# Choosing and loading the first experts one to two steps earlier in a chain of linear attention

## The chip, the cores and the metric

One Trainium2 chip; the kernel runs on one of its cores. The time is the device time of one execution in microseconds (us), the median of a few runs. TensorE (PE) multiplies, VectorE (DVE), ScalarE (ACT) and GpSimd (POOL) do the rest, SyncE (SP) issues most of the DMAs; each of them works through a queue of its own in program order.

## The reference

Three stages follow each other. The first is a linear attention with a state (a delta rule) over 4 batches, 8 heads, 768 tokens and 48 channels; the second sends each of its 3072 rows to one of 8 experts; the third is a dense layer with three inputs and a maximum.

```
for t in range(S):
    y[:, :, t] = einsum('bhd,bhde->bhe', q[:, :, t], state)
    v_old = einsum('bhde,bhd->bhe', state, kt)
    state = state + bt * einsum('bhd,bhe->bhde', kt, vt - v_old)
...
e_idx = argmax(x @ w_gate, axis=1)
out[mask] = gate_w * eom[mask, e] * (maximum(x[mask] @ w1[e], 0) @ w2[e])
...
h = maximum(maximum(x @ w1, x @ w2), x @ w3); return h @ w_out
```

## The kernel before

**The chain.** The attention goes over the tokens in 24 steps of 32 tokens for all heads and batches. A step first multiplies keys and queries with the state (`c_ks`, `c_qs`), takes R = scaled values minus the product on VectorE (L321), multiplies R with a small triangular inverse TT (`c_u`), copies the result from PSUM to Ubd on ScalarE and VectorE (L348, L350), updates the state (`c_s`) and copies it to Sbd (L367, L369); only then can the next step begin. In the texts R(21) is the start of L321 in step 21. The values of step i+2 are scaled on GpSimd at the end of step i (`vscale`, L308): it needs the load of TT(i+2) and of kv(i+2) and stands in GpSimd's queue behind whatever was put there before.

**Routing beside the chain.** Every four steps give 512 rows. Their logits, the choice of an expert and the place in the expert's list are worked out in the steps that follow (`r_g`, L417 to L437, with four additions to the running count `cum` on GpSimd, L433; `r_p`, L445 to L467). Then four indirect DMAs, `r_s` (L474), scatter row number, weight and token into a table in DRAM. Each of them waits on GpSimd until the one before has landed, since both write `tab`.

**Experts ahead of time.** After 12 steps the two experts with most rows so far are taken as the first (`first`, ten small operations on VectorE); their numbers are read into SP registers (`first_values`, L805). SP then loads the raw weights in thirds of 128x1024 numbers (0.5 MB): w1 of the first expert, its w2, and w1 of the second (`raws`, L680). GpSimd splits each third or quarter into a high and a low part with a cast (L696) and a subtraction (L697). SP reads the first 256 list entries of each of the two experts (`lists`, L824; this waits for the scatters), and GpSimd gathers 2 x 128 rows for each (`rows`, L840). Near the end of the chain these rows are turned (`turn`, L855) and multiplied (`m1`); the multiplications of the expert stage then follow without a gap. The raw tile of the second expert's w1 uses the same buffer as that of the first expert's w2, so its load waits until the last quarter of that is split.

**What sets the order.** A table of numbers in `ahead`: the whole part of a number is a step of the chain, its fraction the place within the step. The list is sorted and merged into the step's instructions; the scaling of values comes at the end of a step, behind all of that.

```
fl += [lambda: s.loadT(i + 2), lambda: s.vscale(i + 2)]
```

Of the kernel before, what the change touches and what calls it, by code (L numbers as in the profile page):

```python
# [22 lines left out]
def merge(*lists):  # L23

    items = []
    for li, l in enumerate(lists):
        n = len(l)
        for j, f in enumerate(l):
            items.append(((j + 0.5) / n, li, j, f))
    items.sort(key=lambda t: t[:3])  # L30
    return [t[3] for t in items]


class Attn:
# [9 lines left out]
    def __init__(s, ctx, tc, psum, big, hp, gp, kqt, knv, bt, wgt, xd, tab, ctab, cum, ident, wrm, x2):  # L44
        s.tc, s.nc, s.psum, s.big, s.hp, s.gp = tc, tc.nc, psum, big, hp, gp
        nc = tc.nc
        s.kqt, s.knv, s.btd, s.wgtd, s.xd, s.tab, s.ctab, s.cum = kqt, knv, bt, wgt, xd, tab, ctab, cum
        s.ident, s.wrm, s.ones, s.x2 = ident, wrm, wrm[:, 0:128], x2
        s.NI = 24
        s.NP = 12  # L50
        s.NSL = 6
        s.RLB = "m"
        s.XB, s.xTs, s.RLK = 1, {}, 0
        s.CUT = 0.95
        s.NL = 4
        s.NA = 20
        s.LATE = 0.4
        s.W = (0, 1, 0)
        s.END = 13
        s.TU, s.TB, s.MF = (22.92, 22.95, 22.97), "TRT", 2  # L60

        s.BUD = (5.0, 5.6, 4.6, 5.0)

        s.ORD = {0: 0, 1: 14, 2: 36, 3: 50, 4: 66, 5: 80}
        s.prep = (2.8, 2.2, 1.5, 0.6)
        cp = s.cp = ctx.enter_context(tc.tile_pool(name="acst", bufs=1))
        s.p2 = ctx.enter_context(tc.tile_pool(name="ap2", bufs=2))
        s.dr = ctx.enter_context(tc.tile_pool(name="adr", bufs=1, space=DRAM))
        nc.scalar.preload_act_table_set("natural_log_exp_and_others")
        s.chain = False  # L70
        s.RT, s.RD, s.LT = (15.4, (15.9, 0.3), (17.4, 0.35), (21.8, 0.25)), 0.5, ((18.2, 0.45), (19.3, 0.35), (23.0, 0.05))
        s.KQT, s.AT, s.Gd, s.kv, s.TT, s.x, s.inv = {}, {}, {}, {}, {}, {}, {}

    def consts(s):
# [413 lines left out]
    def run(s, pre, tail):  # L488
        nc, NI, NP = s.nc, s.NI, s.NP
        for i in range(s.NL):  # L490
            s.loadKQ(i)
        s.consts()
        s.warm(9)
        A = [lambda p=p, j=j: s.prods(p, j) for p in range(NP) for j in range(2)]
        for k in range(4):
            A[k]()
        s.inv_load(0)
        for f in (s.inv_n1, s.inv_n2, s.inv_n3):
            f(0)
        B = [u[2] for u in s.steps(s.ORD)[:30]]  # L500
        s1 = s.ORD[1]
        for f in merge(B[:s1 // 3], [A[4], A[5]]) + merge(B[s1 // 3:s1 // 2], [A[6], A[7]]):
            f()
        s.inv_load(1)
        s.inv_n1(1)
        for f in merge(B[s1 // 2:s1], [A[8], A[9], lambda: s.inv_n2(1), A[10], lambda: s.inv_n3(1)]):
            f()
        for f in merge(B[s1:], [lambda: s.load32(0), A[11], lambda: s.inv_load(2), s.empty, lambda: s.load32(1)] + A[12:s.NA]):
            f()
        s.inv_end(0)  # L510
        s.warm(8, s.inv[0]["tt"])
        s.inv_store(0)
        s.vscale(0)
        s.vscale(1)

        spr = [[] for _ in range(NI + 1)]
        put = lambda t, f: spr[int(t + 1)].append(((t + 1) % 1, f))
        t, left = [-1.0], [s.BUD[0]]
        s.ends = []

        def take(c):
            while left[0] < c:
                t[0] = int(t[0]) + 1.0 if t[0] >= 0 else 0.0
                left[0] += s.bud(int(t[0]))
            left[0] -= c
            b = s.BUD[0] if t[0] < 0 else s.bud(int(t[0]))
            t[0] = (int(t[0]) if t[0] >= 0 else -1) + min(0.99, max(0, 1 - (left[0] + c) / b))
        for starts in (s.ORD,):
            for st, c, f, en in s.steps(starts)[30:]:
                take(c)  # L530
                put(t[0], f)
                for sl in st:
                    t0 = t[0]
                    for dt, g in zip(s.prep, (s.inv_load, s.inv_n1, s.inv_n2, s.inv_n3)):
                        if sl > 2:
                            put(t0 - dt, lambda g=g, sl=sl: g(sl))
                        elif sl == 2 and g != s.inv_load:
                            put(-1 + (t0 + 1) * (0.3, 0.5, 0.9)[(s.inv_n1, s.inv_n2, s.inv_n3).index(g)], lambda g=g: g(2))
                    s.ends.append(("start", sl, t0))
                for sl in en:  # L540
                    take(1.4)
                    put(t[0], lambda sl=sl: s.inv_end(sl))
                    assert t[0] + s.LATE < 4 * sl - 1, (sl, t[0])
                    put(t[0] + s.LATE, lambda sl=sl: s.inv_store(sl))
                    s.ends.append((sl, t[0]))
        for k, f in enumerate(A[s.NA:]):
            put(0.05 + k * 0.45, f)
        for t, f in pre(s):
            put(t, f)
        s.chain = True  # L550
        for i in range(-1, NI):
            sp = [f for _, f in sorted(spr[i + 1], key=lambda x: x[0])]
            if i < 0:
                for f in sp:
                    f()
                continue
            q, k = i // 4 - 1, i % 4
            x0 = [lambda: s.r_g(q)] if q >= 0 and k == 1 else [lambda: s.r_p(q)] if q >= 0 and k == 2 else []
            f1 = [lambda: (s.x_store(i - 1), s.r_t(i - 1))] if i else []
            f2 = [lambda: s.r_l(q)] if q >= 0 and k == 0 else []  # L560
            s.load32(i + 2)
            if i >= 7:
                s.r_s({19: [0, 1], 20: [2, 3], 21: [], 22: [], 23: [0, 1]}.get(i, [(i - 7) % 4]))
            n = round(len(sp) * s.CUT) if i < 20 else sum(t < s.CUT for t, _ in spr[i + 1])
            wm = lambda k: [lambda: s.warm(s.W[k])]
            fl = [lambda: s.c_ks(i), lambda: s.c_qs(i)] + x0 + wm(0) + merge([lambda: s.c_u(i)] + f1, sp[:n]) + wm(1)
            fl += [lambda: s.c_s(i)] + merge([lambda: s.c_y(i)] + f2, sp[n:]) + wm(2)
            fl += [lambda: s.loadT(i + 2), lambda: s.vscale(i + 2)]
            for f in fl:
                f()  # L570
        tail(s)
# [54 lines left out]
class Moe:  # L626
# [397 lines left out]
    def ahead(s, a):  # L1024

        G = s.nc.gpsimd
        v = {}

        def later(key, n, t, d):
            def go(j):  # L1030
                if (key, n) not in v:
                    v[key, n] = s.split(key, n, G, G)
                v[key, n][j]()
            return [(t + d * j, lambda j=j: go(j)) for j in range((3, 4)[n])]

        def lists():
            s.ids(0)
            s.ids(1)

        def rows(k):  # L1040
            for c in range(2):
                s.gather(k, c)

        def turned():
            z = [a.p2.tile([128, 1024], F32R, tag="Z", name=f"xT0{j}", bufs=4) for j in range(2)]
            s.xT[0] = [tuple(z[c // 2][:, (c % 2 * 2 + j) * 256:(c % 2 * 2 + j) * 256 + 256] for j in range(2)) for c in range(3)]

        def turn(c):
            if c == 0:
                turned()  # L1050
            s.xpose(0, c, a.TB[c])
        def raws(key, n, slot, t, d):
            us = s.raws(key, n, lambda: s.btile(slot, f"r{n}_{key}", F32), 3)
            return [(t + d * j, u) for j, u in enumerate(us)]
        out = [(a.RT[0], s.first), (a.RT[0] + a.RD, s.first_values), (19.3, s.parts), (21.0, lists),
               (21.3, lambda: rows(0)), (21.6, lambda: rows(1))]
        for (key, n, slot), (t, d) in zip(((0, 0, 0), (0, 1, 1), (1, 0, 1)), a.RT[1:]):
            out += raws(key, n, slot, t, d)
        for (key, n), (t, d) in zip(((0, 0), (0, 1), (1, 0)), a.LT):
            out += later(key, n, t, d)  # L1060
        out += [(t, lambda c=c: turn(c)) for c, t in enumerate(a.TU)]
        out += [(23.1 + 0.1 * f, lambda f=f: s.m1(0, f)) for f in range(a.MF)]
        return out
# [207 lines left out]
```

## Time and profile before

| | |
|---|---|
| Time, median of 3 runs (lowest to highest) | 845.05 us (841.39 to 845.97) |
| The profiled execution: its own time, its span | 841.33 us, 839.6 us |
| Busy PE, DVE, ACT, POOL | 88%, 56%, 35%, 27% of the span |
| Mean granted TensorE clock | 0.93 |

The span is counted from the first to the last instruction. The chain's steps 0 to 23 lie in the first third, to about 273 us; behind it TensorE is nearly always busy. The granted clock is a share of TensorE's full speed, so 1.00 is the upper of its two levels and 0.50 the lower.

### The profile page before, as it was taken

To read this page: it belongs to the slowest core of one execution; us is meant where nothing else is said; L and a number is where in the kernel's file an instruction comes from. 1 tells how busy PE (TensorE), PEld (TensorE's weight loads), DVE (VectorE), ACT (ScalarE), POOL (GpSimd) and SP (SyncE) were. 2 spreads that over 40 slices of the span, in tenths; PEclk is the share of its full clock that TensorE was granted. 3 is DMA by queue.
4 is the path that set the end of the run, shared out by engine and by line. 5 is a ranking of instruction groups with operands and counts; after the bars stand their busy time and mean duration, and the time that the engine had idled before them with its cause. 6 is when DMAs were issued, how large, how long until landed. Compare 5 with 4: busy or idle time off the path is not lost. (4 is left out here: it accounts for less than half of the span.)

```text
span 839.6 us, 20331 instructions
## 1 busy us (share of the span) xinstructions
PE 742.9 (88%) x8506; PEld 635.5 (76%) x8517; DVE 471.0 (56%) x1164; ACT 297.2 (35%) x675; POOL 228.5 (27%) x322
## 2 busy tenths in 40 slices
PE   6746877878776986999899999999999999999996
PEld 4634554555554986999899999889898898988886
DVE  3998999986544532788677795452322313233130
ACT  2213666664342331555354453222221221212111
POOL 5666456422688322034032100001001010100101
PEclk7557899999997999899899999999999999999998
DMA  8894544447634235677766697542010020000001
GB/s 218 214 218 122 144 125 121 102 126 202 169 73 140 85 77 150 235 252 221 250 207 229 235 318 269 196 185 85 10 47 29 1 76 0 29 10 10 28 1 41
DMA packets 86045, 110.28 MB, mean 131 GB/s; under 512 B 53893, under 2 KB 67148, under 8 KB 83388
## 3 DMA queue, kind: packets, MB, share of 16 engines
q1 hardware_dynamic: 57547, 87.08, 33.7%
q10 hardware_dynamic: 19360, 11.42, 5.7%
q0 software_dynamic: 9040, 10.42, 4.1%
q8 instruction: 69, 1.13, 0.6%
q14 instruction: 29, 0.23, 0.1%
HBM read 79.53 MB, written 29.36 MB: 130 GB/s over the span
## 5 line engine op out<-in xcount | busy, mean ns | idle before, releaser
L867 PE MATMUL pm<-xhm,wm 128*128 128x512 f32 x648 | 204.7, 395 | 0.0
L940 DVE TENSOR_TENSOR work<-work,pm 128x512 f32<-128x512 f32 x72 | 49.5, 688 | 175.2 <-PE pm L867 175.2
L867 PEld LDWEIGHTS pm<-xhm,wm 128*128 128x128 f32 x648 | 121.8, 188 | 29.1
L867 PE MATMUL pm<-xlm,wm 128*128 128x512 f32 x324 | 128.1, 396 | 0.0
L953 POOL DMA_INDIRECT out_dram<-work,idm x24 | 23.6, 985 | 332.3 <-ACT work L952 318.0
L840 POOL DMA_INDIRECT xg<-xd,ids x32 | 44.1, 1377 | 142.7 <-PE pt L855 122.1
L942 ACT CAST hmh<-work 128x512 fp32r<-128x512 f32 x36 | 22.4, 621 | 154.3 <-DVE work L940 154.3
L239 DVE TENSOR_TENSOR zt<-Z 128x30 f32<-128x30 f32 (+14 forms) x219 | 73.2, 373 | 3.2 <-POOL Z L218 2.6
L867 PE MATMUL pz<-wm,hmh 128*128 128x384 f32 x320 | 73.7, 334 | 0.0
L867 PEld LDWEIGHTS pm<-xlm,wm 128*128 128x128 f32 x324 | 60.9, 188 | 14.4
L245 DVE TENSOR_TENSOR Z<-Z,zt 128x30 f32<-128x30 f32 (+14 forms) x219 | 69.0, 355 | 0.0
L348 ACT COPY Ubd<-pU 32x192 f32<-32x192 f32 x148 | 45.8, 309 | 62.1 <-PE pU L340 50.2
L360 PE MATMUL pS<-Ubd,kv 128*48 128x192 f32 x368 | 42.8, 363 | 17.9 <-ACT Ubd L348 13.9
L867 PEld LDWEIGHTS pz<-wm,hmh 128*128 128x128 f32 x320 | 57.2, 188 | 0.5
L164 PE MATMUL pg<-KQT 48*32 48x64 f32 x1536 | 40.6, 291 | 18.6 <-DMA KQT<-in_kqt_dram 16.1
L164 PEld LDWEIGHTS pg<-KQT 48*32 48x32 f32 x1536 | 34.5, 151 | 25.9 <-issue 12.2
L360 PEld LDWEIGHTS pS<-Ubd,kv 128*48 128x48 f32 x368 | 22.9, 133 | 37.8 <-ACT Ubd L348 22.9
L902 ACT COPY y<-po 128x256 f32<-128x256 f32 (+6 forms) x30 | 13.3, 445 | 75.7 <-PE po L867 74.1
L367 ACT COPY Sbd<-pS 48x384 f32<-48x384 f32 x72 | 34.0, 472 | 12.0 <-PE pS L360 10.3
L859 DVE TENSOR_TENSOR xl<-pt,xh 128x256 fp32r<-128x256 f32 (+6 forms) x27 | 14.0, 520 | 42.2 <-ACT xh L858 33.2
L867 PE MATMUL pz<-wm,hml 128*128 128x384 f32 x112 | 37.4, 334 | 0.0
L891 ACT ACTIVATE hh<-ph 128x440 fp32r<-128x440 f32 (+5 forms) x48 | 23.8, 503 | 27.0 <-PE ph L867 26.5
(302 smaller groups left out, 1615.1 us busy)
## 6 DMA issues: line engine op xcount, KB each, us to landing
raw<-in_w_dram SPq DMA_DIRECT2D x12, 1536.0 KB
kv<-in_knv_dram SPq DMA_DIRECT2D x24, 384.0 KB
wd<-work SPq DMA_DIRECT2D x24, 384.0 KB
wm<-wd SPq DMA_DIRECT2D x8, 1152.0 KB
KQT<-in_kqt_dram ACTq DMA_DIRECT2D x20, 448.0 KB
xd<-x SPq DMA_DIRECT2D x24, 192.0 KB
r<-in_w_dram SPq DMA_DIRECT2D x9, 512.0 KB
raw<-x SPq DMA_DIRECT2D x6, 768.0 KB
```

The costliest lines, as they stand in the source:

```text
L164: nc.tensor.matmul(ps[b * 32:b * 32 + 32, o:o + 64], kq[:, 0, :], kq.rearrange("p k t -> p (k t)"), start=True, stop=True, tile_position=( ...
L239: nc.vector.tensor_mul(t, Z[:, a:e, m].unsqueeze(2).to_broadcast([128, e - a, n]), Z[:, m, m + 1:].unsqueeze(1).to_broadcast([128, e - a, n]))
L245: nc.vector.tensor_add(Z[:, a:e, m + 1:], Z[:, a:e, m + 1:], t)
L348: nc.scalar.copy(dst, src)
L360: nc.tensor.matmul(s.pS[q][j * 64:j * 64 + 48, g2 * 192:g2 * 192 + 192], s.kv[i][:, 0, h, :], s.Ubd[h // 4][:, h % 4, :], start=(i == 0 an ...
L367: nc.scalar.copy(dst, src)
L840: s.nc.gpsimd.indirect_dma_start(t[0:r.ct], None, s.xd[0:2049] if k < 2 else s.xd, bass.IndirectOffsetOnAxis(s.gid[k][0:r.ct, c, 0:1], 0))
L867: s.nc.tensor.matmul(ps, a, b, start=(start and k == 0), stop=(stop and k == n - 1))
L891: nc.scalar.activation(hi, ps, AF.Relu)
L940: nc.vector.tensor_max(m, m, ps)
L942: nc.scalar.copy(hi, m)
L953: nc.gpsimd.indirect_dma_start(s.out, bass.IndirectOffsetOnAxis(i[:, c, 2:3], 0), y, None, bounds_check=3071, oob_is_err=False)
```

## The change

Only numbers of the table change, and the list of scatters by step. `first` goes from 15.4 to 14.2, `first_values` from 15.9 to 14.7 (RT's first number and RD). The raw thirds of w1 go from 15.9 to 14.8, those of w2 from 17.4 to 16.0, those of the second expert's w1 from 21.8 to 19.0. Their splits (LT) go from 18.2, 19.3 and 23.0 to 16.1, 17.3 and 21.0. The count of rows goes from 19.3 to 18.3, the lists from 21.0 to 20.4, the gathers from 21.3 and 21.6 to 20.8 and 21.2. The four scatters of the fourth routing, two each in steps 19 and 20 before, are all issued in step 19.

```diff
--- before.py
+++ after.py
@@ -68,7 +68,7 @@
         s.dr = ctx.enter_context(tc.tile_pool(name="adr", bufs=1, space=DRAM))
         nc.scalar.preload_act_table_set("natural_log_exp_and_others")
         s.chain = False
-        s.RT, s.RD, s.LT = (15.4, (15.9, 0.3), (17.4, 0.35), (21.8, 0.25)), 0.5, ((18.2, 0.45), (19.3, 0.35), (23.0, 0.05))
+        s.RT, s.RD, s.LT = (14.2, (14.8, 0.3), (16.0, 0.25), (19.0, 0.25)), 0.5, ((16.1, 0.4), (17.3, 0.35), (21.0, 0.2))
         s.KQT, s.AT, s.Gd, s.kv, s.TT, s.x, s.inv = {}, {}, {}, {}, {}, {}, {}
 
     def consts(s):
@@ -560,7 +560,7 @@
             f2 = [lambda: s.r_l(q)] if q >= 0 and k == 0 else []
             s.load32(i + 2)
             if i >= 7:
-                s.r_s({19: [0, 1], 20: [2, 3], 21: [], 22: [], 23: [0, 1]}.get(i, [(i - 7) % 4]))
+                s.r_s({19: [0, 1, 2, 3], 20: [], 21: [], 22: [], 23: [0, 1]}.get(i, [(i - 7) % 4]))
             n = round(len(sp) * s.CUT) if i < 20 else sum(t < s.CUT for t, _ in spr[i + 1])
             wm = lambda k: [lambda: s.warm(s.W[k])]
             fl = [lambda: s.c_ks(i), lambda: s.c_qs(i)] + x0 + wm(0) + merge([lambda: s.c_u(i)] + f1, sp[:n]) + wm(1)
@@ -1052,8 +1052,8 @@
         def raws(key, n, slot, t, d):
             us = s.raws(key, n, lambda: s.btile(slot, f"r{n}_{key}", F32), 3)
             return [(t + d * j, u) for j, u in enumerate(us)]
-        out = [(a.RT[0], s.first), (a.RT[0] + a.RD, s.first_values), (19.3, s.parts), (21.0, lists),
-               (21.3, lambda: rows(0)), (21.6, lambda: rows(1))]
+        out = [(a.RT[0], s.first), (a.RT[0] + a.RD, s.first_values), (18.3, s.parts), (20.4, lists),
+               (20.8, lambda: rows(0)), (21.2, lambda: rows(1))]
         for (key, n, slot), (t, d) in zip(((0, 0, 0), (0, 1, 1), (1, 0, 1)), a.RT[1:]):
             out += raws(key, n, slot, t, d)
         for (key, n), (t, d) in zip(((0, 0), (0, 1), (1, 0)), a.LT):
```

The first place is GpSimd's queue at steps 18 to 20, from the scaling of kv20 to that of kv21 and one row on (kv and TT bear the step's number, w1_0 is the first expert's w2, tab the table, xg0 gathered rows). Before:

```order
L308 TENSOR_TENSOR kv20_4240<-kv20_4240,TT20_4380 128x384
L474 DMA tab_78<-rdat3_4290,rpos3_4299 25600x3 x2
L696 CAST w0_0h_4344<-r0_0_3938 128x1024
L697 TENSOR_TENSOR w0_0l_4345<-r0_0_3938,w0_0h_4344 128x1024
L696 CAST w1_0h_4473<-r1_0_4203 128x768
L697 TENSOR_TENSOR w1_0l_4474<-r1_0_4203,w1_0h_4473 128x768
L308 TENSOR_TENSOR kv21_4383<-kv21_4383,TT21_4509 128x384
```

With the change:

```order
L308 TENSOR_TENSOR kv20_4255<-kv20_4255,TT20_4398 128x384
L474 DMA tab_78<-rdat3_4305,rpos3_4314 25600x3 x4
L308 TENSOR_TENSOR kv21_4401<-kv21_4401,TT21_4519 128x384
L840 DMA xg0_0_4612<-xd_76,ids0_4602 128x384
L840 DMA xg0_1_4614<-xd_76,ids0_4602 128x384
```

The pieces of splitting between kv20 and kv21 are gone from here (all of them stand before kv20 now), and four scatters stand there in place of two.

The second place is the same queue at steps 20 to 23 (w0_1 is the second expert's w1, cum the running count, xg1 the rows of the second expert). Before:

```order
L308 TENSOR_TENSOR kv22_4512<-kv22_4512,TT22_4643 128x384
L433 TENSOR_TENSOR cum_74<-cum_74,rohb4_4698 128x8 x4
L840 DMA xg0_0_4754<-xd_76,ids0_4708 128x384
L840 DMA xg0_1_4756<-xd_76,ids0_4708 128x384
L840 DMA xg1_0_4758<-xd_76,ids1_4710 128x384
L840 DMA xg1_1_4760<-xd_76,ids1_4710 128x384
L308 TENSOR_TENSOR kv23_4646<-kv23_4646,TT23_4795 128x384
L459 COPY rdat4_4845<-xrow_199 128x4
L460 COPY rdat4_4845<-tok_194 128x4
L474 DMA tab_78<-rdat4_4845,rpos4_4854 25600x3 x2
L696 CAST w0_1h_4985<-r0_1_4769 128x1024
L697 TENSOR_TENSOR w0_1l_4986<-r0_1_4769,w0_1h_4985 128x1024
```

With the change:

```order
L308 TENSOR_TENSOR kv22_4522<-kv22_4522,TT22_4655 128x384
L433 TENSOR_TENSOR cum_74<-cum_74,rohb4_4710 128x8 x4
L696 CAST w0_1h_4720<-r0_1_4443 128x1024
L697 TENSOR_TENSOR w0_1l_4721<-r0_1_4443,w0_1h_4720 128x1024
L840 DMA xg1_0_4766<-xd_76,ids1_4604 128x384
L840 DMA xg1_1_4768<-xd_76,ids1_4604 128x384
L308 TENSOR_TENSOR kv23_4658<-kv23_4658,TT23_4805 128x384
```

The pair of cast and subtraction stands twice more between the last gather and the scaling of kv23 (left out here). All three thirds of the second expert's w1 are thus split ahead of kv23, where they stood behind it.

The third place is SP's queue at steps 14 to 16 (r0_0 is the raw w1 of the first expert, x the rows that the chain stores). Before:

```order
L302 DMA TT16_3830<-td4_172 128x8x33
L294 DMA kv17_3833<-in_knv_dram 128x768
L805 TENSOR_LOAD early_92 x2
L384 DMA xd_76<-x14_3828 128x384
L680 DMA r0_0_3938<-in_w1_dram 128x1024
L302 DMA TT17_3964<-td4_172 128x8x33
L294 DMA kv18_3967<-in_knv_dram 128x768
```

With the change:

```order
L805 TENSOR_LOAD early_92 x2
L384 DMA xd_76<-x13_3692 128x384
L680 DMA r0_0_3824<-in_w1_dram 128x1024
L302 DMA TT16_3850<-td4_172 128x8x33
L294 DMA kv17_3853<-in_knv_dram 128x768
L384 DMA xd_76<-x14_3848 128x384
L302 DMA TT17_3966<-td4_172 128x8x33
L294 DMA kv18_3969<-in_knv_dram 128x768
```

Two more thirds of r0_0 stand on the two sides of x14 (left out). TT16 moved behind the read of the experts' numbers and the first raw third, and TT17 behind all three thirds instead of one.

## Rows read from the trace of the kernel before

**Rows 1.** Busy time by step of the chain, from one R to the next, all engines.
```profile
202.34:209.43 7.09, 6.07 (x188) 4.42 (x177) 3.08 (x7) 3.31 (x9) 1.85 (x2) 1.00 0.99 308
...
242.98:252.75 9.77, 6.14 (x165) 4.15 (x166) 4.54 (x17) 3.36 (x10) 8.05 (x8) 1.00 0.10 24
...
252.75:267.88 15.13, 9.41 (x155) 5.87 (x158) 6.85 (x21) 3.14 (x8) 11.39 (x16) 0.66 0.55 180
```

**Rows 2.** Timeline of VectorE, the R of steps 22 and 23.
```profile
252.75 0.55 DVE L321 TENSOR_TENSOR R<-kv,pR 128x384 f32<-128x384 f32 x1 [3.98 <-POOL kv L308]
...
267.88 0.56 DVE L321 TENSOR_TENSOR R<-kv,pR 128x384 f32<-128x384 f32 x1
```

**Rows 3.** Timeline of TensorE in step 22: first transpose of the gathered rows.
```profile
261.04 1.04 PE L855 MATMUL pt<-ident,xg 128*128 128x128 f32 x2 [2.55 <-DMA xg<-xd,ids]
```

**Rows 4.** Timeline of VectorE: step 14, the choice of experts in step 15, step 18.
```profile
190.79 0.17 DVE L467 CAST rpos<-rpf 128x4 int32<-128x4 f32 x1
...
195.80 0.15 DVE L713 COPY row<-pcnt 1x8 f32<-1x8 f32 x1
...
197.78 0.16 DVE L744 CAST early<-row 1x2 int32<-1x2 f32 x1
...
220.83 2.13 DVE L467 CAST rpos<-rpf 128x4 int32<-128x4 f32 x1
```

**Rows 5.** Timeline of SyncE's DMA issues: raw parts, lists, raw load after the chain.
```profile
199.42 0.36 SPq L680 DMA_DIRECT2D r<-in_w_dram  x1
...
248.85 0.99 SPq L824 DMA_DIRECT2D ids<-tab  x2
...
282.55 1.43 SPq L680 DMA_DIRECT2D raw<-in_w_dram  x3
...
300.76 1.76 SPq L824 DMA_DIRECT2D ids<-tab  x2
```

**Rows 6.** Timeline of GpSimd, steps 16 to 23.
```profile
206.11 0.83 POOL L308 TENSOR_TENSOR kv<-kv,TT 128x384 f32<-128x384 f32 x1 [8.54 <-DMA TT<-td]
...
220.61 2.33 POOL L697 TENSOR_TENSOR w_0l<-r,w_0h 128x1024 fp32r<-128x1024 f32 x1
...
236.75 0.82 POOL L696 CAST w_0h<-r 128x768 fp32r<-128x768 f32 x1
...
242.10 0.84 POOL L308 TENSOR_TENSOR kv<-kv,TT 128x384 f32<-128x384 f32 x1
...
252.67 1.03 POOL L433 TENSOR_TENSOR cum<-cum,rohb 128x8 bf16<-128x8 bf16 x4
...
255.19 0.97 POOL L840 DMA_INDIRECT xg<-xd,ids  x1 [0.30 <-issue]
...
264.16 1.04 POOL L696 CAST w_1h<-r 128x1024 fp32r<-128x1024 f32 x1
...
267.60 1.04 POOL L696 CAST w_1h<-r 128x1024 fp32r<-128x1024 f32 x1
```

**Rows 7.** Timeline of GpSimd: scatters to the table, then a gather.
```profile
243.10 1.03 POOL L474 DMA_INDIRECT tab<-rdat,rpos  x1 [0.15 <-issue]
...
245.56 0.96 POOL L474 DMA_INDIRECT tab<-rdat,rpos  x1 [1.43 <-DMA tab<-rdat,rpos]
...
283.42 1.00 POOL L474 DMA_INDIRECT tab<-rdat,rpos  x1 [1.92 <-DVE row L713]
...
290.29 0.97 POOL L474 DMA_INDIRECT tab<-rdat,rpos  x1 [5.87 <-DMA tab<-rdat,rpos]
...
296.84 0.97 POOL L474 DMA_INDIRECT tab<-rdat,rpos  x1 [1.92 <-DMA tab<-rdat,rpos]
...
304.01 0.99 POOL L840 DMA_INDIRECT xg<-xd,ids  x1 [6.21 <-ACT y L902]
```

**Rows 8.** Busy time of two stretches of 4 us, all engines.
```profile
258.00:262.00 4.00, 1.13 (x4) 0.70 (x5) 1.41 (x4) 1.24 (x4) 2.82 (x5) 0.50 0.76 294
...
266.00:270.00 4.00, 3.93 (x151) 3.14 (x144) 2.90 (x7) 1.50 (x5) 3.92 (x3) 1.00 0.14 51
```

## The prediction

> **What bounds the kernel now.** I first read the busy time by step of the chain, since the change touches nothing else. A step is a loop of dependences over TensorE, VectorE and ScalarE, so its length, not anyone's busy time, is what counts. Step 16, without a stall, takes 7.09 us even with the DMA engines full at 308 GB/s; step 21 takes 9.77 and step 22 takes 15.13, the latter at a mean granted clock of 0.66 [rows 1]. So 2.7 and 8.0 us, 10.7 together, lie above a plain step there; that is all that the change can win at its end of the chain. (Step 21 also carries a routing, so not all of its excess is a stall.) The timelines say what the stalls are. R of step 22 waited 3.98 us for GpSimd's scaling of kv22 [rows 2], because the splitting of w2 stood in front of it. Then TensorE waited 2.55 us at the first transpose for gathered rows [rows 3]. Behind R of step 23, at 267.88, TensorE has a long row of multiplications and is the bound. Whatever moves R(23) moves the end by as much.
>
> **What the change removes.** The split of w2 and the gathers are to be over before step 22. If nothing took their place, R(21) would come one plain step after another and the wait for rows would be gone.
>
> **What it adds, part by part.**
>
> *The choice of experts in step 14.* The routing of step 14 holds VectorE until 190.96; the choice took from 195.80 to 197.94 in step 15 [rows 4], 2.1 us. Now it comes right behind the routing, so it ends at about 193.1. VectorE's copies of Ubd stand behind it in step 14 and no longer in step 15, so 2.1 us go in and up to as much comes back: between 0 and 2.1; I take 1.2, as the routing already uses up the slack of step 14. R(16) would be at 202.34 + 1.2, about 203.5. On SP, x13, the first raw third, TT16 and kv17 wait behind the read of the experts' numbers. Before, the first third was issued at 199.42 [rows 5], 1.5 us after the choice; so it goes out at 194.6 now.
>
> *The load of TT17.* GpSimd's scaling of kv17 began at 206.11, when TT17 had landed [rows 6]: 6.7 us behind the issue of the one raw third that stood in front of it. Now all three thirds, TT16, kv17 and x14 do. At the least TT17 lands 6.7 us after the first third again, at 201.3; with some 1.8 MB more (1.05 of raw weights, the rest kv17, x14 and TT16) at the 308 GB/s of step 16, 5.8 us more, at 207.1. I take 205.0, nearer to the upper end because these bytes go through the same queue in front of it.
>
> *GpSimd's queue from there to kv20.* Scalings at 0.84, scatters at 1.2 with the gap before them, the four additions 1.0, a third of w1 3.44 (264.16 to 267.60), two quarters of w2 5.35 (236.75 to 242.10) [rows 6, 7]. In the order of the change up to the scaling of kv20: four scalings 3.4, three scatters 3.6, three thirds 10.3, four additions 1.0, four quarters 10.7, together 29.0. So kv20 is scaled at 234.0. A chain of plain steps from 203.5 wants R(20) at 231.9, so GpSimd is by then the later of the two.
>
> *Four scatters in step 19.* Each waits for the one before to land. In a quiet stretch the second began 2.46 us after the first; a group of four with a 1.5 MB raw load issued 0.9 us ahead of it ran from 283.42 to 297.81, 14.4 us, its second one waiting 5.87 [rows 5, 7]. Bounds: 3 x 2.46 + 0.96 = 8.3, and 14.4. Here the three raw thirds of the second expert go out as soon as the last quarter of w2 is split, one scaling before the first scatter. That is the case of the second group almost exactly, so I take 14.4: the last scatter ends at 248.5. Behind it in the queue stand the scaling of kv21, which R(21) needs (it ends at 249.3, where plain steps would have R(21) at 239.0), and the gathers.
>
> *Lists and gathers.* SP reads the lists once the last scatter has landed: 2.3 us after it (246.52 to 248.85). Until the rows can be asked for, between 1 us (what the issue of both lists took) and 3.25 us pass (300.76 to 304.01, with GpSimd idle) [rows 5, 7]. I take 3.25. So the first gather starts at 254.1. On SP, x19, TT22 and kv23 wait behind the lists; TT22 is needed only after the gathers. Two gathers at 0.97 + 0.30 are 2.5, up to 256.6.
>
> *The queue up to kv23.* Scaling of kv22 to 257.4, additions to 258.5, a third to 261.9, two gathers to 264.4, two thirds (6.9) to 271.3, scaling of kv23 to 272.1. This is the new wait: in the kernel before the three thirds stood behind kv23 and cost nothing there. Counted from the additions of step 21 it is 12.8 us before that scaling can begin, where two plain steps from R(21) = 249.3 would have R(23) at 263.5. R(23) thus comes at 272.1, 4.2 us later than 267.88, and TensorE stands idle before it for some 8 us.
>
> *The clock.* In the stall of step 22 the granted clock fell to 0.50 (258 to 262), the lower level, after a stretch in which TensorE did little; by 266 to 270 it was 1.00 again [rows 8]. There the lower level met a chain that waits anyway; behind R(23) it would meet TensorE's own work. From TensorE's first transpose at 261.04 to full clock by 266 at the latest are up to 4.9 us at half speed, 2.4 us of work lost; the lower bound is nothing. I take 1.5, since the first microseconds are still chain.
>
> *The shared operand port.* In step 18 a cast of four numbers per partition took VectorE 2.13 us instead of 0.17 [rows 4] and ended at 222.96, when GpSimd's subtraction beside it ended, at 222.94 [rows 6]. In the change the thirds of w1 run from about 207 to 217, beside the routing of step 17, which has five operations from SBUF alone. By that one row this costs some 2 us in step 17. The Trainium skill, page "SBUF — State Buffer", section "SBUF: two separate sides", says that VectorE (with two SBUF inputs, or in a mode that uses two ports) and GpSimd lock a common pair of ports for a whole instruction, and the other blocks; by it each of the five could wait for one piece of splitting, up to about 5 us. By either the sum stays as it is, as GpSimd is the later one; but the rule takes away from the chance that the chain runs plain, which the second rival needs.
>
> **Sum.** 4.2 + 1.5 = +5.7 us. The profiled execution took 841.33 (span 839.6 and 1.7 around it), so 847.0 for one like it; the median of before lies 3.7 above that one, so 850.8 beside it, 0.7% slower.
>
> **Rivals.**
>
> *No difference.* The scatters land quickly (8.3 us instead of 14.4): kv23 is scaled at 266.0, R(23) is 1.9 earlier than before, and with about 1 us for the clock the time is 844.2. For it: three thirds are soon through if SP gets to them early. Against: they can't go before w2's last quarter is split, and that is just ahead of the scatters.
>
> *Faster.* GpSimd keeps up: TT17 lands at 201.3, the scatters take 8.3, the rows can be asked for after 1 us. Then 6.1 + 3.7 + 2.3, 12.1 us, go from the sum, kv23 is scaled at 260.0, no long idle stretch falls before it, and R(23) is 7.9 earlier: 837.2. For it: 10.7 us of stalls are really there to be won. It decides from R(23) at 263.7 on, 8.4 below my sum, so it needs quick scatters and one of the other two. Against: even then the 12.8 us ahead of kv23 leave no slack in two steps.
>
> *Later still.* The second group's 5.87 us wait comes twice, or TT17 at 207.1: 3 to 5 us more, 853.8 to 855.8.
>
> **How the numbers follow.** Forecast 0.50, no difference 0.31, faster 0.15, later still 0.04. A measurement of this kernel can tell about 0.5%, 4.2 us. Slower than that: most of the forecast's and all of the last, 0.48. Within it: the second case and the forecast's lower edge, 0.36. Faster: 0.16. The range goes from 840, short of the far end of the faster case, to 856; the forecast's own is 847 to 855.
>
> **What would show it.** Right: in step 23 VectorE's R waits for GpSimd's scaling for several us, R(23) lies behind 268, step 22 itself is near 8 us from R(22) and has no wait for gathered rows; four scatters take over 12 us with R(21) waiting behind them; the clock is low just behind R(23). Wrong: R(23) without a wait on GpSimd, or four scatters within 9 us; if both hold, the faster rival stands. A stall in steps 15 to 18 longer than 8 us would mean that the chain, not GpSimd, set the time.

## The result and the profile after

| | before | after |
|---|---|---|
| Median of 8 runs each (lowest to highest) | 842.86 us (841.23 to 845.97) | 848.25 us (841.96 to 852.75) |
| Ratio, 95% interval | | 1.0064 (1.0037 to 1.0092) |
| The profiled execution: its own time, its span | 841.33 us, 839.6 us | 841.96 us, 840.2 us |

The change makes the kernel slower by 0.64%, 5.4 us of the medians. The profiled execution after is the quickest of its eight, so its span says little; the chain in it can be read all the same.

Busy time by step of the chain from one R to the next, then by stretches of 4 us, of the kernel after. The columns are those of [rows 1]: us, then TensorE, its weight loads, VectorE, ScalarE and GpSimd, the granted clock, the DMA share and GB/s.

```profile
210.42:225.39 14.97, 7.87 (x174) 5.42 (x176) 9.66 (x17) 3.37 (x10) 14.23 (x15) 0.82 0.28 63
...
240.61:250.82 10.21, 6.42 (x216) 5.01 (x205) 3.08 (x8) 3.41 (x9) 3.73 (x4) 0.99 0.24 64
250.82:258.81 7.99, 7.38 (x143) 4.92 (x147) 4.53 (x16) 3.37 (x10) 3.80 (x8) 0.58 0.72 179
258.81:272.12 13.31, 8.75 (x204) 5.52 (x196) 8.74 (x21) 3.15 (x8) 12.61 (x10) 0.87 0.21 66
...
266.00:270.00 4.00, 3.46 (x84) 2.20 (x82) 1.97 (x5) 0.48 (x1) 3.92 (x3) 0.78 0.14 50
270.00:274.00 4.00, 1.27 (x67) 1.20 (x68) 0.87 (x2) 0.56 (x2) 3.39 (x5) 1.00 0.01 3
274.00:278.00 4.00, 4.00 (x43) 3.36 (x42) 1.95 (x6) 2.36 (x7) 0.98 (x1) 1.00 0.05 5
```

Step 22, from R(22) to R(23), takes 13.31 us and GpSimd is busy for 12.61 of them. In steps 21 and 22 together, 21.30 us against 24.90 in [rows 1], the steps do get 3.6 us shorter. But R(21), where they begin, is 7.8 us late by then (250.82 against 242.98). Step 17 takes 14.97 us (8.11 before, from 209.43 to 217.54), again with GpSimd busy for nearly all of it; of that 4.8 us are left at R(20) (240.61 against 235.79), and the wait for the scatters adds the other 3.0 in step 20. VectorE's timeline of the kernel after, the choice of experts, the routing in step 17 and R of steps 21 to 23, with TensorE's first transpose of gathered rows:

```profile
190.09 0.15 DVE L713 COPY row<-pcnt 1x8 f32<-1x8 f32 x1
...
191.70 0.16 DVE L744 CAST early<-row 1x2 int32<-1x2 f32 x1
...
213.17 1.93 DVE L423 TENSOR_TENSOR rd<-rl,rm 128x32 f32<-128x32 f32 x1
215.14 0.94 DVE L425 SCALAR_TENSOR_TENSOR rsel<-rd,wts 128x32 f32<-128x32 f32 x1
...
216.34 2.17 DVE L429 TENSOR_TENSOR roh<-wts,rr 128x32 f32<-128x32 f32 x1
218.54 0.75 DVE L431 CAST rohb<-roh 128x32 bf16<-128x32 f32 x1
...
250.82 0.56 DVE L321 TENSOR_TENSOR R<-kv,pR 128x384 f32<-128x384 f32 x1 [4.88 <-POOL kv L308]
...
258.81 0.55 DVE L321 TENSOR_TENSOR R<-kv,pR 128x384 f32<-128x384 f32 x1 [0.72 <-POOL cum L433]
...
260.36 0.44 PE L855 MATMUL pt<-ident,xg 128*128 128x128 f32 x2
...
272.12 0.55 DVE L321 TENSOR_TENSOR R<-kv,pR 128x384 f32<-128x384 f32 x1 [3.20 <-POOL kv L308]
```

In [rows 2] R waited for GpSimd's scaling in step 22 and not in step 23. Now it waits in step 21 (4.88 us) and in step 23 (3.20 us), and R(23) lies at 272.12 instead of 267.88. The wait for gathered rows of [rows 3] is gone: the first transposes stand at 260.36 without a wait. GpSimd's timeline of the kernel after, from the scaling of kv17 to the end of the chain:

```profile
204.04 0.83 POOL L308 TENSOR_TENSOR kv<-kv,TT 128x384 f32<-128x384 f32 x1 [2.75 <-DMA TT<-td]
207.15 1.01 POOL L474 DMA_INDIRECT tab<-rdat,rpos  x1 [2.27 <-DMA tab<-rdat,rpos]
208.16 1.04 POOL L696 CAST w_0h<-r 128x1024 fp32r<-128x1024 f32 x1
...
212.71 2.35 POOL L697 TENSOR_TENSOR w_0l<-r,w_0h 128x1024 fp32r<-128x1024 f32 x1
...
234.38 0.84 POOL L308 TENSOR_TENSOR kv<-kv,TT 128x384 f32<-128x384 f32 x1
235.38 1.03 POOL L474 DMA_INDIRECT tab<-rdat,rpos  x1 [0.15 <-issue]
242.44 0.96 POOL L474 DMA_INDIRECT tab<-rdat,rpos  x1 [6.03 <-DMA tab<-rdat,rpos]
245.16 0.96 POOL L474 DMA_INDIRECT tab<-rdat,rpos  x1 [1.76 <-DMA tab<-rdat,rpos]
248.95 0.96 POOL L474 DMA_INDIRECT tab<-rdat,rpos  x1 [2.84 <-DMA tab<-rdat,rpos]
249.93 0.86 POOL L308 TENSOR_TENSOR kv<-kv,TT 128x384 f32<-128x384 f32 x1
254.03 1.01 POOL L840 DMA_INDIRECT xg<-xd,ids  x1 [3.25 <-DMA ids<-tab]
...
271.25 0.84 POOL L308 TENSOR_TENSOR kv<-kv,TT 128x384 f32<-128x384 f32 x1
...
284.15 0.97 POOL L474 DMA_INDIRECT tab<-rdat,rpos  x1 [2.70 <-DMA tab<-rdat,rpos]
285.14 1.04 POOL L433 TENSOR_TENSOR cum<-cum,rohb 128x8 bf16<-128x8 bf16 x4
```

This is the queue that the prediction added up: four scatters from 235.38 to 249.91 with the second one waiting 6.03 us for the first to land, kv21 right behind them, 3.25 us of waiting for the lists ahead of the first gather, and kv23 behind the thirds of w1. SyncE's DMA issues of the kernel after, the first raw third and the raw load behind the chain, the latter at 282.55 in [rows 5]:

```profile
193.34 0.36 SPq L680 DMA_DIRECT2D r<-in_w_dram  x1
...
287.48 1.41 SPq L680 DMA_DIRECT2D raw<-in_w_dram  x3
```

The chain thus ends 4.9 us later, 4.2 of it at R(23). The rest, 0.7 us, comes from the four scatters that stand behind kv23 in both kernels and start with its scaling: with the change the last of them lands just ahead of the additions to `cum` at 285.14, which the last routing needs. Before, these additions (280.21) waited for VectorE's routing and not for a scatter.

### The profile page after: what moved, and what is told of

The parts are those of the page before. It is cut to its first block, busy times and chain, and to the rows that moved or that the text cites. A ratio compares the mean times of both kernels' runs of the same rounds, so it can differ in the third digit from the quotient of the medians.

```text
span 840.2 us, 20335 instructions
## 1 busy us (share of the span) xinstructions
PE 744.4 (89%) x8504; PEld 637.0 (76%) x8517; DVE 477.3 (57%) x1164; ACT 298.3 (36%) x675; POOL 227.9 (27%) x322
## 5 line engine op out<-in xcount | busy, mean ns | idle before, releaser
L867 PEld LDWEIGHTS pm<-xlm,wm 128*128 128x128 f32 x324 | 60.9, 188 | 14.4
L360 PE MATMUL pS<-Ubd,kv 128*48 128x192 f32 x368 | 45.1, 381 | 22.2 <-ACT Ubd L348 11.4
L164 PE MATMUL pg<-KQT 48*32 48x64 f32 x1536 | 43.0, 303 | 18.7 <-DMA KQT<-in_kqt_dram 14.4
L164 PEld LDWEIGHTS pg<-KQT 48*32 48x32 f32 x1536 | 36.6, 158 | 26.0 <-issue 13.3
```

What stands on the lines that cost most here:

```text
L164: nc.tensor.matmul(ps[b * 32:b * 32 + 32, o:o + 64], kq[:, 0, :], kq.rearrange("p k t -> p (k t)"), start=True, stop=True, tile_position=( ...
L360: nc.tensor.matmul(s.pS[q][j * 64:j * 64 + 48, g2 * 192:g2 * 192 + 192], s.kv[i][:, 0, h, :], s.Ubd[h // 4][:, h % 4, :], start=(i == 0 an ...
L867: s.nc.tensor.matmul(ps, a, b, start=(start and k == 0), stop=(stop and k == n - 1))
```

## The experiments

The theory is that of the prediction: GpSimd's queue up to the scaling of kv23 sets R(23), and with it the end. The rivals are that the early choice and loads cost the time, that the routing held up in step 17 does, or that four scatters in one step do. Edits are shown against the kernel after unless a line says otherwise, and ratios are those to the kernel before; e0 was run once, the others in five rounds beside the kernel before. The medians of before in the three groups of runs were 840.58, 841.63 and 840.8 us.

### e1: the third of w1 behind kv23 again

```diff
-s.LT = ((16.1, 0.4), (17.3, 0.35), (21.0, 0.2))
+s.LT = ((16.1, 0.4), (17.3, 0.35), (23.0, 0.05))
```

> The changed kernel, with the split of the second expert's first weight put back to step 23, behind the scaling of kv23. Theory (GpSimd's queue up to kv23 sets R of step 23): kv23 is scaled right behind the second pair of gathers, at about 262 instead of 271.25, and R(23) comes 4 to 6 us earlier than 272.12, at 266 to 268. The thirds then stand ahead of the last two scatters and of the additions of the last routing, which wait for them, so that only 1 to 3 us of this reach the end: 0.2 to 0.4% faster than the changed kernel, about the time of the kernel before (+0.2 to +0.5%). Rival (the 15 us that step 17 takes, with VectorE blocked beside the splitting of w1, are what the change costs): R(23) stays at 272.

Measured 841.0 us, ratio to before 1.0010 (0.9978 to 1.0042). Timeline of e1, GpSimd, VectorE and SyncE:

```profile
260.90 0.85 POOL L308 TENSOR_TENSOR kv<-kv,TT 128x384 f32<-128x384 f32 x1
...
268.70 0.55 DVE L321 TENSOR_TENSOR R<-kv,pR 128x384 f32<-128x384 f32 x1
...
283.33 1.41 SPq L680 DMA_DIRECT2D raw<-in_w_dram  x3
```

kv23 is scaled 10.4 us earlier than after, R(23) has no wait left, and the raw load comes 4.15 us earlier. In the same rounds e2, which keeps that split where the change put it, took 848.12 us. One pair of numbers in the table takes back the loss: the split of the second expert's w1 ahead of kv23 is its cause, and what is left of the change, the early choice and loads and the four scatters, costs nothing that the interval shows. R(23) came 0.7 later than expected; the raw load gained more than expected, 3.4 us at R(23) and 0.7 behind it, where the tail of scatters is short again.

### e2: two scatters in step 19 and two in step 20

```diff
-s.r_s({19: [0, 1, 2, 3], 20: [], 21: [], ...
+s.r_s({19: [0, 1], 20: [2, 3], 21: [], ...
```

> The changed kernel, with the four scatters of the fourth routing two and two in steps 19 and 20 again. Theory: R(21) no longer waits for all four and comes about 3 us earlier (247.5 instead of 250.82), but the lists, the gathers and everything behind them in GpSimd's queue end when they did, so R(22) gains at most 1 us and R(23) stays within 1 us of 272.1; no difference in time from the changed kernel (+0.5% to +0.8% over the kernel before). Rival (each stall of the chain counts by itself): the 3 us gained at R(21) arrive at R(23), 269, and the time is 0.35% less than the changed kernel's.

Measured 848.12 us, ratio 1.0095 (1.0062 to 1.0127). Timeline of e2, VectorE:

```profile
249.83 0.55 DVE L321 TENSOR_TENSOR R<-kv,pR 128x384 f32<-128x384 f32 x1 [1.63 <-issue]
...
273.15 0.55 DVE L321 TENSOR_TENSOR R<-kv,pR 128x384 f32<-128x384 f32 x1 [4.33 <-POOL kv L308]
```

R(21) no longer waits for kv21, which was scaled by 245.04, but it wins only 1.0 us where I had expected 3, and R(23) is 1.0 later than after. Two executions of the changed kernel itself differ by 1.25 us at R(21) (249.57 in e0 below), so neither is a difference that one trace can show. R(20) came 1.2 us later here (241.83), and step 20 took 8.00 us without any wait for GpSimd: the chain, held up in step 17, is by then about as late as GpSimd. The last scatter ends at 249.00 (249.91 after): the four need their round trips one after another wherever they stand in the queue. That they are in one step is not the cost.

### e3: the splits of the first expert later

```diff
-s.LT = ((16.1, 0.4), (17.3, 0.35), (21.0, 0.2))
+s.LT = ((17.5, 0.15), (18.2, 0.2), (21.0, 0.2))
```

> The changed kernel, with the split of the first expert's w1 behind the routing of step 17 (17.5 on, instead of 16.1 on) and that of its w2 in step 18. VectorE's routing in step 17 then has no splitting beside it. Theory (the queue counts, not the block in step 17): step 17 falls from 14.97 us to 8 to 9.5, so R(18) comes about 6 us earlier, but GpSimd idles before the additions of step 17 and its queue ends about 4 us later than with the change: R(23) at 275 to 277, slower than the changed kernel by 0.3 to 0.5%. Rival (the block in step 17 is the cost): R(23) at 265 to 267, faster than the changed kernel by 0.6%.

Measured 850.89 us, ratio 1.0147 (1.0092 to 1.0201). Timeline of e3, VectorE:

```profile
219.37 0.55 DVE L321 TENSOR_TENSOR R<-kv,pR 128x384 f32<-128x384 f32 x1 [0.72 <-POOL w_0l L697]
...
255.12 0.55 DVE L321 TENSOR_TENSOR R<-kv,pR 128x384 f32<-128x384 f32 x1 [9.66 <-POOL kv L308]
...
276.18 0.55 DVE L321 TENSOR_TENSOR R<-kv,pR 128x384 f32<-128x384 f32 x1 [3.20 <-POOL kv L308]
```

Step 17 is short again (8.41 us, from 210.96) and R(18) comes 6.0 us earlier than after, but GpSimd begins its first split at 215.71 instead of 208.16. R(21) then waits 9.66 us for kv21, and R(23) falls at 276.18, inside the 275 to 277 expected. Of the 6.0 us little is left at R(20) (239.80, 240.61 after), since the splitting now runs beside the routing of step 18, which takes 12.44 us (8.93 after). So e3 moved the block rather than removed it; what it shows is that R(23) follows GpSimd's queue. The longest step of the profile after was not what the time hung on, and the rival on step 17, which had R(23) at 265 to 267, falls; e1 speaks against it too, with the time of the kernel before although its step 17 takes 14.10 us.

### e7: all three moves that the queue suggests

```diff
-s.LT = ((16.1, 0.4), (17.3, 0.35), (21.0, 0.2))
+s.LT = ((15.6, 0.1), (17.3, 0.35), (23.0, 0.05))
-s.r_s({19: [0, 1, 2, 3], 20: [], ...
+s.r_s({19: [0, 1], 20: [2, 3], ...
-(20.4, lists), (20.8, lambda: rows(0)), (21.2, lambda: rows(1))
+(21.0, lists), (21.3, lambda: rows(0)), (21.6, lambda: rows(1))
```

> A version put together from the theory: the changed kernel, with the split of w1 ahead of the scaling of kv17 (15.6 on), so that it is over before the routing of step 17; scatters two and two, lists and gathers as in the kernel before (21.0, 21.3, 21.6); the second expert's split behind kv23. Theory: step 17 takes 8 to 9.5 us, R(17) waits 1 to 2 us for kv17, neither R(21) nor R(22) nor R(23) waits for GpSimd by more than 1 us, and R(23) comes at 258 to 262, 6 to 10 us before that of the kernel before; 2 to 5 us of that may be lost again behind it, where the thirds stand ahead of the last scatters: 0.4 to 0.9% faster than the kernel before. Rival (the early raw loads themselves cost, by holding up the small loads or TensorE's instructions): R(18) at 222 or later as with the change, and no gain over the kernel before.

Measured 836.97 us, ratio 0.9975 (0.9942 to 1.0008): at least as good as before, and well ahead of after, but less than the 0.4 to 0.9% faster that I had expected. With w1 split ahead of step 17's routing, step 17 takes 7.25 us; R(17) waits 3.81 us for kv17, where I had 1 to 2, and R(21) comes at 245.81. R(23), expected at 258 to 262, came only at 266.68. Timeline of e7, GpSimd, TensorE and VectorE in steps 21 and 22:

```profile
248.75 0.85 POOL L308 TENSOR_TENSOR kv<-kv,TT 128x384 f32<-128x384 f32 x1
...
252.36 1.02 POOL L840 DMA_INDIRECT xg<-xd,ids  x1 [1.78 <-DMA ids<-tab]
...
255.12 0.39 PE L331 MATMUL pY<-Sbd,KQT 112*32 112x96 f32 x4 [0.35 <-issue]
...
258.06 0.87 PE L331 MATMUL pY<-Sbd,KQT 112*32 112x96 f32 x12 [0.40 <-issue]
...
258.23 0.56 DVE L321 TENSOR_TENSOR R<-kv,pR 128x384 f32<-128x384 f32 x1 [4.90 <-POOL kv L308]
```

The trace names kv as R(22)'s releaser, but kv22 was scaled at 248.75. While the four gathers run (252.36 to 257.15) TensorE goes through one product in groups of a few matmuls with 0.35 to 0.4 us of "issue" between them, and R starts 0.17 us after the last group does. This is a product of the queries (L331); the product that R itself takes in (L318) had ended by 254.01 in the trace, so why R follows the later one is open.

### e8: e7 with the second pair of gathers in step 22

The edit is shown against e7.

```diff
-(21.3, lambda: rows(0)), (21.6, lambda: rows(1))
+(21.3, lambda: rows(0)), (22.5, lambda: rows(1))
```

> The version of three moves, with the gathers of the second expert's rows in step 22 (22.5) instead of step 21. In the three-move run R(22) came at 258.23, since TensorE crept through the last products ahead of it in pieces of four to six for 4 us, while four gathers of 128 rows ran. Theory (four gathers at once hold up TensorE's instructions): with two gathers there at most 2 us of that remain, R(22) comes at 253.5 to 256, R(23) at 261 to 264 instead of 266.68, and the time is 0.2 to 0.5% below that of the three moves, 0.4 to 0.8% below the kernel before. Rival (the creeping has to do with the place in the program, not with the gathers): R(22) stays at 258, no difference from the three moves.

Measured 837.96 us, ratio 0.9966 (0.9933 to 0.9999). Timeline of e8, TensorE and VectorE in steps 21 and 22:

```profile
255.16 0.39 PE L331 MATMUL pY<-Sbd,KQT 112*32 112x96 f32 x5 [0.38 <-issue]
...
255.27 0.55 DVE L321 TENSOR_TENSOR R<-kv,pR 128x384 f32<-128x384 f32 x1 [2.81 <-issue]
...
258.06 0.41 PE L340 MATMUL pU<-R,TT 32*32 32x48 f32 x6 [0.37 <-issue]
```

R(22) came at 255.27 as expected, 0.11 us behind the start of TensorE's last group and ahead of the next end of a scaling (254.77 + 0.84 = 255.61), so by the times it is TensorE that it follows. R(23) came at 267.92 instead of 261 to 264: the slow stretch was not shortened but cut in two, one behind each pair of gathers (252.31 and 256.02). The time is about that of e7, where 0.2 to 0.5% less was expected.

### e9: the kernel before, with that one move alone

The edit is that of e8, made in the kernel before.

> The kernel before, with only the gathers of the second expert's rows in step 22 (22.5) instead of step 21 (21.6). In the kernel before TensorE crept through the products of step 22 from 253.6 to 258.5 and then waited 2.55 us for the first expert's rows at 261.04. Theory (four gathers at once, beside the raw load of the second expert, hold up TensorE's instructions): the creeping is shortened by 2 us or more and the first rows land earlier, the first transpose starts at 257.5 to 259.5, R(23) comes at 264.5 to 266.5 instead of 267.88, time 0.15 to 0.4% below the kernel before. Rival (the raw load of 1.5 MB at 252 to 257 does it): creeping and first transpose stay as they are, within 1 us.

Measured 840.82 us, ratio 0.9982 (0.9957 to 1.0006). Timeline of e9, GpSimd and TensorE:

```profile
259.11 1.02 POOL L840 DMA_INDIRECT xg<-xd,ids  x1 [0.15 <-DVE rsm L455]
...
260.39 0.29 PE L340 MATMUL pU<-R,TT 32*32 32x48 f32 x4 [0.49 <-issue]
...
262.98 0.69 PE L855 MATMUL pt<-ident,xg 128*128 128x128 f32 x2
```

The first transpose stands at 262.98, later than the 261.04 of [rows 3] and than I expected, and R(23) at 270.26, where I had 264.5 to 266.5; the time is that of the kernel before within the interval. My idea that gathers pulled apart would free TensorE falls in both runs.

### e4: the kernel before, with the choice and the first expert's loads early

```diff
-s.RT = (15.4, (15.9, 0.3), (17.4, 0.35), (21.8, 0.25))
+s.RT = (14.2, (14.8, 0.3), (16.0, 0.25), (21.8, 0.25))
```

> The kernel before, with only the choice of experts and the raw loads of the first expert's two weights early (14.2, 14.8, 16.0); splits, scatters, lists, gathers and the second expert's load as before. Theory (not the loads but GpSimd's queue costs time): the choice adds 1 to 2 us in step 14 or 15, kv17 is scaled at 204 to 206 as with the change, step 17 takes 8 to 9 us since no splitting runs beside its routing, and the splits end when they did: R(23) within 2 us of 267.88 and no difference in time from the kernel before (within 0.3%). Rival (the early loads themselves cost, through late small loads or late instructions): R(18) at 220 or later, R(23) at 271 or later, slower by 0.4% or more.

Measured 836.23 us, ratio 0.9952 (0.9916 to 0.9987), where I had expected no difference beyond 0.3%. The rival that early loads cost time falls, though one of its marks was met: R(18) came at 220.56, 3.0 us later than before, and R(23) at 267.00, as early as the theory had it. The gain is not in the chain of the profiled execution: the raw load behind it is issued at 284.49, 1.9 us later than before, and from there to the end of the span it takes 550.8 us (557.1 in the profile before). That stretch differs by up to 7 us between single traces, so this pair does not say where the gain of the medians comes from. It is open.

### e10: e1 with the second expert's raw thirds issued late

The edit is shown against e1.

```diff
-s.RT = (14.2, (14.8, 0.3), (16.0, 0.25), (19.0, 0.25))
+s.RT = (14.2, (14.8, 0.3), (16.0, 0.25), (21.8, 0.25))
```

> The changed kernel with the second expert's split behind kv23 (as in the first experiment), and its raw load back at 21.8, behind the lists, so that no 1.5 MB load runs beside the four scatters of step 19. Theory (the raw load makes the scatters slow): the four take 8.3 to 10.5 us instead of 14.5, kv21 is scaled at 244 to 246, R(21) comes at 247 to 248.5 without a wait for it, the first gather starts at 248 to 250 instead of 254, R(22) at 255 to 256.5. At R(23) some of it may be lost again, as the raw load then runs beside the gathers: 264 to 268. Rival (each scatter waits 3 to 4 us whatever runs beside it): the four take 12 to 14 us.

Measured 839.46 us, ratio 0.9996 (0.9966 to 1.0026). Timeline of e10, GpSimd's four scatters:

```profile
236.20 1.03 POOL L474 DMA_INDIRECT tab<-rdat,rpos  x1 [0.15 <-issue]
239.20 0.96 POOL L474 DMA_INDIRECT tab<-rdat,rpos  x1 [1.97 <-DMA tab<-rdat,rpos]
241.60 0.96 POOL L474 DMA_INDIRECT tab<-rdat,rpos  x1 [1.44 <-DMA tab<-rdat,rpos]
246.81 0.96 POOL L474 DMA_INDIRECT tab<-rdat,rpos  x1 [4.25 <-DMA tab<-rdat,rpos]
```

Without the 1.5 MB of raw weights beside them the four take 11.6 us (14.5 after, 13.1 in e1), and the second waits 1.97 instead of 6.03. But the fourth waits 4.25, so the sum lies between what the load (8.3 to 10.5) and what the scatters themselves (12 to 14) would give: the load is part of it, how large a part stays open. The marks behind the scatters were missed: R(21) came at 249.46, the first gather at 252.16, R(22) at 257.71 and R(23) at 268.80, each 0.8 us or more later than expected. Ahead of R(22) GpSimd waited 2.40 us with the scaling of kv22 for the load of TT22, which stands behind the lists on SP.

### e0: the change once more

> The changed kernel once more, for a second trace. In the first trace the raw load behind the chain was issued 4.9 us later than in the kernel before, but the span was only 0.6 us longer, while the median of the times differs by 5.4. Theory: up to that load the execution repeats within 1.5 us (R(23) at 271 to 273.5, the load at 286 to 289), and what lies behind it varies from execution to execution by several us whatever the kernel, so that this second trace has a span of 842 to 850. Rival: the part behind the chain is shorter with the change, by some 4 us, every time: span 839 to 841.

Measured 847.63 us, span 845.8: as expected, and the rival (839 to 841) falls. VectorE's R of step 23, then busy time by stretches of 4 us around it:

```profile
271.01 0.56 DVE L321 TENSOR_TENSOR R<-kv,pR 128x384 f32<-128x384 f32 x1 [4.67 <-POOL kv L308]
```

```profile
266.00:270.00 4.00, 0.67 (x34) 0.46 (x24) 0.34 (x1) 0.00 (x0) 3.92 (x3) 1.00 0.10 34
270.00:274.00 4.00, 2.38 (x67) 2.10 (x68) 1.10 (x3) 0.95 (x4) 2.28 (x5) 0.60 0.01 0
274.00:278.00 4.00, 4.00 (x21) 3.88 (x20) 1.29 (x4) 1.16 (x3) 1.55 (x2) 0.55 0.04 4
```

Here TensorE works for 0.67 us of the 4 just ahead of R(23) and stands still for 4.95 us in one piece (3.27 in the first profile after), and the granted clock is 0.60 and 0.55 in the two stretches behind it. From R(23) to the raw load (288.50) are 17.5 us. Before it was 14.7; in the first profile after, where the clock was 1.00 at once, it was 15.4, and there the tail of scatters is in it. In e0 that tail cost nothing: the additions to `cum` waited another 4.20 us for VectorE. R(21) and R(22) came 1.25 and 2.3 us earlier than in the first profile after (249.57 and 256.49), and R(21) waited 1.99 us instead of 4.88.

## Why the prediction was right

**The queue to kv23.** The mechanism came as forecast: four scatters took 14.5 us (14.4 predicted), R(21) waited behind them, the three thirds stood ahead of kv23, and R(23) came at 272.12 (272.1). That it agrees to 0.1 us is luck: two errors cancel on the way, and in e0 the same kernel has R(23) at 271.01. The scaling of kv20 ended at 235.22, 1.2 us later than my 234.0, the last scatter at 249.91 (248.5), and R(21) came at 250.82 (249.3). Then the lists were issued at 251.08, 1.2 us behind the last scatter where I had 2.3, and the first gather came 2.95 us after that where I had 3.25, so that it stood at 254.03 (254.1) again. I had no wait for TT22 ahead of kv22 either; it was 0.44 us here and 2.40 in e10. The rows that the sum rested on, the second group of scatters above all [rows 7], were the right ones. e1 and e3 show that this queue is the cause: shorten it ahead of kv23 and the loss is gone, start it later and R(23) moves with it. e2 shows that the scatters cost what they cost in any place.

**The chain beside it.** I had R(20) at 231.9, with GpSimd the later one. It was the other way round: R(20) came at 240.61, without a wait, 5.4 us behind the end of kv20's scaling, chiefly because step 17 took 14.97 us, 7.9 more than a plain step. I had put some 2 us there, and those not into the sum. Four operations of the routing took 5.8 us together, each ending within 0.05 us of a GpSimd instruction (the first at 213.17 + 1.93 = 215.10, the split at 212.71 + 2.35 = 215.06). The Trainium skill, page "SBUF — State Buffer", section "SBUF: two separate sides", has VectorE (with two SBUF inputs, or in a mode that uses two ports) and GpSimd lock a common pair of ports for a whole instruction; the trace agrees, with 0.75 to 2.17 us for each of the four operations, about 0.2 us each in the kernel before. That is 5.0 us more than they took there, the size that the prediction had by the Trainium skill. The error did not reach the sum, as R(21) then waited another 4.88 us behind the scatters. But it was close: in e0 that wait is 1.99 us, and the sign that I had named for the chain setting the time, a stall of more than 8 us in steps 15 to 18, was missed by little.

**The choice in step 14.** It ran from 190.09 to 191.86, 1.8 us, and the first raw third went out at 193.34 (194.6 predicted). I took 1.2 us out of bounds of 0 to 2.1 for what it costs the chain; R(16) came 0.3 later than before (202.66, 202.34), 0.8 in e0 (203.16) and 2.4 in e4 (204.76). The scaling of kv17 began 1.0 us earlier than I had it (204.04 for 205.0), but the scatter behind it waited 2.27 us for the one before, which I had not in the sum; that is where the 1.2 us at kv20 come from.

**The clock.** I added 1.5 us for a low clock behind R(23). In the first profile after there was none. In e0 it was there, at 0.60 and 0.55: from R(23) to the raw load it took 2.8 us more than before. In e2 (274 to 278) and e3 (278 to 282) the stretch behind R(23) shows 0.59 as well, with 1.7 and 2.15 us more. So the term holds in three of four executions with this wait. I had TensorE idle for some 8 us before R(23); it was 3.3 to 5.0 us, and since R waits as long in e3 as in the first profile after (3.20), that length alone does not tell the two apart. What does is open.

**Step 22.** "Near 8 us from R(22)" was wrong: the sum had R(22) at 257.4 and R(23) at 272.1, so my own numbers gave 14.7; 13.31 were measured.

**Sum.** Predicted +5.7 us; the medians differ by 5.4. In the first trace the raw load moves by 4.9: 4.2 at R(23), nothing from the clock, and 0.7 from the tail of scatters that I did not count. In e0 it moves by 5.95: 3.1 at R(23) and 2.8 behind it, with the low clock. So the sum is right in size, and its split into 4.2 and 1.5 is met by neither trace. That the span of the profiled pair differs by 0.6 only comes from behind the chain: the shift is 4.9 us at the raw load and 0.4 by 426 us, and the part from the raw load to the end took 557.1 us before and 552.7 after, but 557.3 in e0. Of the rivals, "no difference" needed scatters in 8.3 us, and no run had four in that; "faster" needed R(23) at 263.7, and not even e7 had that.

**Where the hoped-for gain went.** The stall on kv22 of 3.98 us and the wait for rows of 2.55 [rows 2, 3] were really won. A wait of 4.88 us on kv21 and one of 3.20 on kv23 (1.99 and 4.67 in e0) took their places, with the routing of step 17 held up besides. e7 and e8 take away the split ahead of kv23 and the one beside the routing, and are a little ahead of before (0.25%, with an interval that reaches past 1, and 0.34%). But e4, which has neither the early splits nor the other moves, is 0.48% ahead, so it is not shown that those moves gain anything over the early loads alone. In e7 and e8 TensorE's slow stretch beside the gathers stands where the rest of the gain was expected; neither of the two runs that moved gathers away from it gained by that.

## What to carry to other kernels

Before moving work earlier, write down the whole in-order queue that it joins, with durations from the trace, up to the next instruction that the critical chain waits for; here that sum gave R(23) to 0.1 us in one execution and to 1.1 in another, although the chain beside it did something else. The thirds of w1 were free behind that instruction; ahead of it they put off kv23 by 10.4 us and R(23), once the slack was used up, by 3.4 (e1 against after). The longest step in a profile need not be the one that sets the time: e3 shortened it by 6.6 us, and R(23) came 4.1 us later. A sum can agree to a tenth because two errors in it cancel; it pays to compare every mark on the way, and starts with starts.

## What the runs showed of the hardware

- An indirect scatter that must wait for the one before started 2.4 to 4.1 us after it in most places. Around the issue of a raw load of 1.5 MB the first such pair took 4.8 to 7.2 us from start to start (7.06 after, 7.24 in e0, 4.80 in e4), in e3 the second pair 5.98 too. Four pairs took 4.9 to 5.2 us without such a load beside them (before at 227.31, after at 275.52, e8 at 272.96, e10 at 241.60).
- Around gathers of 128 rows TensorE issued in groups of mostly 1 to 9 matmuls about 0.75 us apart, for 2 to 4 us, in before, e1, e7, e8, e9 and e10. Beside the gathers of after, e0, e2 and e3 it did not. Where the groups show, TensorE was at the products with small tiles (L340, 32x48, or L331, 112x96); beside the gathers without them it was at others. In e4 there is one gap of 1.10 us instead, and single groups of this kind stand beside scatters too (e0 at 235.34 and 236.08). So gathers alone do not bring them about, and moving gathers can put them beside other products, as in e8 and e9; the mechanism was not tried.
- The stretch from the raw load behind the chain to the end of the span took between 550.2 (e7) and 557.5 us (e1) in eleven traces, a part that no edit touches. Its spread is larger than the change's effect, so single spans could not have decided anything here.
